# Attention rows stored whole and loaded in 512-byte pieces, w_ch1 in 128-column tiles, and new orders for the head and the middle

## Chip, core and metric

The kernel runs on one core of one Trainium2 chip. The metric is the device time of one execution in microseconds; the time given is the median of three runs. TensorE multiplies matrices, VectorE (DVE), ScalarE (ACT) and GpSimd (POOL) do the elementwise work, and SyncE (SP) issues most of the DMA transfers, ACT a few.

## The reference

Two parts follow each other, all in float32. The first is attention over a small memory, for 8 batches with 8 heads, 576 tokens, head size 64 and 32 memory slots:

```
a    = softmax over tokens of phi                  # 576 x 32 per head
k_m  = a^T k ;  v_m = a^T v                        # 32 x 64 per head
attn = softmax over slots of (q k_m^T / 8)         # 576 x 32 per head
x    = attn v_m, heads side by side                # 576 x 512 per batch
```

The second is a mixer on x:

```
u   = x + (relu(x^T w_tok1) w_tok2)^T              # over tokens, 576 -> 256 -> 576
out = u + relu(u w_ch1) w_ch2                      # over channels, 512 -> 1536 -> 512
```

## The kernel before

**Numbers.** Nearly all products run on operands split into a high and a low part (names with h and l), three products for one. The weights arrive as 64-bit words, from which ACT and DVE make the two parts in place (lines 825 to 859: raww for the token weights, rawc for the channel weights).

**Units of work.** A quad is half of a batch, four heads. Attention and the token mixer run by quad, 16 in all. The channel mixer runs by chunk of 512 tokens, 9 in all.

A quad's steps, in the order in which one waits for another:

- load phi, k and v, and q. For batches from 2 on the phi maxima are taken apart: load phi turned (l. 629), reduce it, store the maxima to DRAM (l. 638) and load them on all partitions as r (max_in, l. 644); GpSimd subtracts them (phi_sub, l. 647), and ACT takes the exponential (l. 446);
- k_m and v_m (kvp, l. 452), then the scores sp (l. 492). DVE turns them, so that a partition holds a token of a block of 32 for one head, and makes the softmax S with an exponential on ACT (l. 514) in between;
- two uses of S. Turned back it becomes aT, from which ACT and DVE make the operands a (l. 717, 722) for x. The token mixer instead needs tokens on partitions and heads side by side. S goes out to a DRAM tile, rows (rows_out, l. 545), and comes back in that layout (rows_in, l. 552 and 555, or 696 and 699 into the tile side). ACT copies it to the high part (nat_high, l. 703) and GpSimd makes the low part (nat_low, l. 711);
- Ap (attn^T w_tok1, l. 566), copied out as Ah by ACT (l. 737) and Al by DVE (l. 741); Rp (l. 749), then its relu parts Rh and Rl; at last the four tiles u (l. 768), each x and the token mixer summed in PSUM.

The channel mixer of chunk c makes cp (l. 146, with w_ch1), its relu parts hh and hl (l. 115, 118), and acc (l. 169, with w_ch2).

**Stages.** The head, to some 120 us, loads and converts all weights, runs the quads of batches 0 and 1 and the first chunk. The middle, to some 372 us, runs the 12 quads of batches 2 to 7 and chunks 1 and 2; u of later chunks is spilled to DRAM (l. 796). The middle also makes the sums of parts of w_ch1 and w_ch2 on which the last stage works, and stores them (class Sums: store_rest, l. 388, writes parts of w_ch1 as they are, store, l. 380, the sums; class Tops, l. 323). The last stage runs chunks 3 to 8 in three pairs with seven products of half size in place of eight (l. 292 and 2285), from u_p (l. 208), the spilled u.

**What sets the order.** All engines take their instructions in program order, and a planner at build time writes that order for head and middle. Each step has an engine, a duration, what it follows and the buffers (rooms) that it takes. The planner takes the engine that can start first, and on it, among the steps that can start within 0.1 us of that, the one with the highest rank; the program's order is that of the planned begins. In the head the ranks are the list RANKS; in the middle they come from a due time written beside each step (todo_at). Transfers are modelled by a line:

```
landed[eng] = max(landed.get(eng, 0.0), z.begin + 2.2) + 0.91 * z.move + 1.6 * (z is slow)
z.ready = max(landed[eng] + margin, z.end + z.tail)
```

so there is a line for each issuing engine, and a transfer counts as ready `margin` after its place in it, or `tail` after its issue. `slack` is added for steps on PE and SP, and `behind` limits how far SP's line may run ahead. In the middle margin is 4.0, slack 0.4 and behind 3.5; rows_in has a tail of 6.0, rows_out and the store of the maxima 2.4, the load of phi turned 4.0 or 8.0. The products of the channel mixer form one chain of steps of low rank.

Of the kernel before, what the change touches and what calls it, by code (L numbers as in the profile page):

```python
# [20 lines left out]
P = 128  # L21
# [7 lines left out]
def kernel(  # L29
# [97 lines left out]
    class Chunk:  # L127
# [6 lines left out]
        def mm_1(s, ps, f, only=None):  # L134
            w = slice(f % 2 * P, (f % 2 + 1) * P)
            c1h, c1l = c1[f // 2]
# [40 lines left out]
        def residual(s, a):  # L177
            if a == 0:
                s.o = wide(F32, "o" + s.n)
            nc.gpsimd.tensor_tensor(  # L180
# [161 lines left out]
    class Sums:  # L342
# [6 lines left out]
        def words(s):  # L349
            t = s.t = wide(F32R, f"sums{s.p}").rearrange("p a n -> p (a n)")  # L350
            s.v = t.rearrange("p (o x m) -> p o x m", o=4, x=2)
            for j in range(2):
                h, l = (f32(t[:, 2 * j : 2 * j + 2]).rearrange("p a (o n) -> p o a n", o=2) for t in c1[s.p])
# [73 lines left out]
    class Quad:  # L427
# [122 lines left out]
        def rows_in(s, tag, bufs):  # L550
            s.raw = sb.tile([P, NC, 4 * M], F32, tag=tag, name="raw" + s.n, bufs=bufs)
            nc.sync.dma_start(
                out=s.raw[:, :FULL], in_=s.rows[: FULL * P].rearrange("(c p) n -> p c n", p=P)
            )
            nc.sync.dma_start(out=s.raw[:TAIL, FULL], in_=s.rows[FULL * P :])
# [53 lines left out]
    class LateQuad(Quad):  # L609
# [84 lines left out]
        def rows_in(s):  # L694
            s.raw = side[0][:, :640].rearrange("p (c n) -> p c n", c=NC)
            nc.sync.dma_start(
                out=s.raw[:, :FULL], in_=s.rows[: FULL * P].rearrange("(c p) n -> p c n", p=P)
            )
            nc.sync.dma_start(out=s.raw[:TAIL, FULL], in_=s.rows[FULL * P :])

        def nat_high(s):
            s.nat_room()
            nc.scalar.copy(out=s.nh[:, :FULL], in_=s.raw[:, :FULL])  # L703
            nc.scalar.copy(out=s.nh[:TAIL, FULL], in_=s.raw[:TAIL, FULL])

        def nat_low(s, eng):
            for o, a, h in (
                (s.nl[:, :FULL], s.raw[:, :FULL], s.nh[:, :FULL]),
                (s.nh[TAIL:, FULL], s.raw[:TAIL, FULL], s.nh[:TAIL, FULL]),
# [194 lines left out]
    class PartC1:  # L904
# [10 lines left out]
        def load(s, raw):  # L915
            nc.sync.dma_start(out=raw.rearrange("p (a n) t -> p a (n t)", a=NKK), in_=w_ch1[s.f // 2])

        def dst(s):
            c1[s.f // 2] = tuple(
                sb.tile([P, NKK, 256], F32R, tag="c1", name=f"c1{x}{s.f}", bufs=NF) for x in "hl"  # L920
# [3 lines left out]
        def pick(s, x):  # L924
            return x.rearrange("p (a n) -> p a n", a=NKK)
# [37 lines left out]
    class Step:  # L963


        def __init__(s, eng, us, fn, after, take, use, move, port, other):
# [4 lines left out]
            s.fill, s.lands, s.not_before, s.tail = 0, False, 0.0, 1.0  # L971
# [13 lines left out]
    def plan(rank, ways, slow=None, slack=0.0, margin=0.85, behind=1e9):  # L985
# [10 lines left out]
        free, taken, landed, port = {}, {}, {}, 0.0  # L996
        left, done = [z for z in steps if not z.after], []

        def when(z):
            t = max(free.get(z.eng, 0.0), port if z.port else 0.0, z.not_before)  # L1000
            if z.eng == "SP":
                t = max(t, landed.get("SP", 0.0) - behind)
            for y in z.after:
                t = max(t, y.end if y.eng == z.eng and not (y.lands or y.move and y.eng == "ACT") else y.ready + slack * (z.eng in ("PE", "SP")))
# [20 lines left out]
        while left:  # L1025
# [1475 lines left out]
```

## Time and profile before

| | |
|---|---|
| median of three runs | 721.59 us (720.98 to 722.43) |
| the profiled execution | 722.78 us, of which span 721.0 us |
| TensorE busy | 708.4 us (98%) |
| DVE, ACT, GpSimd busy | 517.6, 371.4, 88.8 us |
| mean granted TensorE clock | 0.997 |
| DMA packets | 99200, of them 38985 under 512 bytes, 155.26 MB |

The span runs from the first instruction to the last of the profiled execution. A row of the table by stretches gives the stretch and its length in us, the busy time of PE (TensorE's products, with the number of them), PEld (its weight loads, beside the products), DVE, ACT and POOL, then the granted clock of TensorE as a share of 2.4 GHz, the mean busy share of the 16 DMA engines, and GB/s. A busy TensorE may still run at a low clock, so that column is read with it. In a timeline, the bracket at the end is the idle time of the engine before the instruction, and what ended it. The chain of waits is followed back from the last instruction, at each step to what released it; a DMA there runs from its issue to its landing. SPq is SP's queue, in which transfers are issued.

### The profile page before, as it was taken

How to read it: one execution, taken by the hardware profiler on the slowest of the kernel's cores; microseconds unless marked ns; L12 is line 12 of the kernel's file. 1: busy time of each engine (PE TensorE's matmuls, PEld its weight loads, DVE VectorE, ACT ScalarE, POOL GpSimd, SP SyncE). 2: the span in 40 equal slices, each digit the busy share in tenths (PEclk: the TensorE clock that was granted, in tenths of full speed). 3: DMA queues.
4: the chain of work that ended last, by engine and by line, in shares of the span. 5: the costliest groups of instructions: out<-in, count | busy, mean ns of one | idle time of the engine just before them, and what ended most of it. 6: DMA issues, size and time to landing. Idle time of an engine off the chain costs nothing.

```text
span 721.0 us, 11450 instructions
## 1 busy us (share of the span) xinstructions
PE 708.4 (98%) x4317; PEld 591.9 (82%) x4317; DVE 517.6 (72%) x854; ACT 371.4 (52%) x688; POOL 88.8 (12%) x80
## 2 busy tenths in 40 slices
PE   8999999999999998999999999999999999999998
PEld 7778888778888887888888888888888888888887
DVE  4999864877788676687965758966247977426983
ACT  6899765326564555445533465434345443436450
POOL 2143123021212402101400000000000000000000
PEclk9999999999999999999999999999999999999999
DMA  9967342789899999846437876184659065658202
GB/s 356 415 213 290 117 118 79 272 208 303 256 285 287 311 307 329 273 120 205 186 122 224 303 279 244 35 305 155 204 164 332 31 210 175 204 201 289 91 30 87
DMA packets 99200, 155.26 MB, mean 215 GB/s; under 512 B 38985, under 2 KB 65609, under 8 KB 94793
## 3 DMA queue, kind: packets, MB, share of 16 engines
q1 hardware_dynamic: 88632, 121.37, 50.0%
q10 hardware_dynamic: 10512, 33.17, 14.3%
q8 instruction: 34, 0.56, 0.3%
q14 instruction: 22, 0.17, 0.1%
HBM read 117.34 MB, written 37.16 MB: 214 GB/s over the span
## 4 chain that ended last, share of the span: by engine, by line
PE 82%; DMA 8%; DVE 5%; SPq 2%; ACT 1%; issue 1%; POOL 0%; ACTq 0%; POOLq 0%; DVEq 0%
PE ma L292 14%; PE acc L169 12%; PE cp L146 11%; PE mU L2285 10%; PE mB L2285 7%; PE mc L292 7%; PE u L768 5%; PE mD L2285 3%; PE mA L2285 3%; PE mb L292 3%; DMA side<-rows 2%; PE Ap L566 2%; DMA raww<-in_w_tok_dram 2%; PE kvp L452 1%; PE u L582 1%; DMA u_p<-spilled 1%
## 5 line engine op out<-in xcount | busy, mean ns | idle before, releaser
L169 PE MATMUL acc<-hh,c 128*128 128x512 f32 x288 | 100.6, 398 | 0.0
L169 PEld LDWEIGHTS acc<-hh,c 128*128 128x128 f32 x288 | 54.5, 189 | 13.1 <-issue 1.9
L169 PE MATMUL acc<-hl,c 128*128 128x512 f32 x144 | 56.7, 393 | 0.1
L146 PE MATMUL cp<-uh,c1h 128*128 128x512 f32 x144 | 52.4, 404 | 0.0
L146 PE MATMUL cp<-ul,c1h 128*128 128x512 f32 x144 | 50.5, 391 | 0.0
L146 PE MATMUL cp<-uh,c1l 128*128 128x512 f32 x144 | 50.4, 390 | 0.0
L2271 ACT CAST rT<-hid 128x512 fp32r<-128x512 f32 x54 | 32.0, 621 | 27.1 <-PE mB L2285 14.9
L2272 DVE TENSOR_TENSOR rT<-hid,rT 128x512 fp32r<-128x512 f32 x54 | 35.7, 684 | 7.0 <-ACT rT L2271 7.0
L2139 DVE TENSOR_TENSOR hid<-mb,hid 128x512 f32<-128x512 f32 x12 | 8.3, 692 | 41.8 <-ACT hid L2219 41.8
L115 ACT ACTIVATE hh<-cp 128x512 fp32r<-128x512 f32 x36 | 21.5, 598 | 29.9 <-PE cp L146 29.6
L711 POOL TENSOR_TENSOR nat<-side,nat 128x512 fp32r<-128x512 f32 (+1 forms) x24 | 23.5, 981 | 104.2 <-ACT nat L703 80.4
L2142 ACT ACTIVATE hid<-hid 128x512 f32<-128x512 f32 x24 | 15.2, 632 | 35.3 <-DVE hid L2139 35.3
L146 PEld LDWEIGHTS cp<-uh,c1h 128*128 128x128 f32 x144 | 26.6, 188 | 7.7 <-issue 3.6
L146 PEld LDWEIGHTS cp<-uh,c1l 128*128 128x128 f32 x144 | 27.0, 188 | 6.0
L169 PEld LDWEIGHTS acc<-hl,c 128*128 128x128 f32 x144 | 27.4, 190 | 4.9 <-DVE hl L118 0.6
L146 PEld LDWEIGHTS cp<-ul,c1h 128*128 128x128 f32 x144 | 27.1, 188 | 4.6
L118 DVE SCALAR_TENSOR_TENSOR hl<-cp,hh 128x512 fp32r<-128x512 f32 x36 | 24.7, 685 | 7.6 <-ACT hh L115 7.3
L778 ACT COPY side<-u 128x288 f32<-128x288 f32 (+1 forms) x44 | 17.0, 391 | 25.1 <-PE u L768 21.7
L2271 ACT CAST r<-hid 128x512 fp32r<-128x512 f32 x36 | 22.4, 623 | 14.3 <-PE mU L2285 5.4
L768 PE MATMUL u<-w2h,Rh 128*128 128x288 f32 x96 | 27.4, 301 | 0.6 <-ACT side L778 0.6
L2272 DVE TENSOR_TENSOR r<-hid,r 128x512 fp32r<-128x512 f32 x36 | 24.7, 685 | 4.6 <-ACT r L2271 4.3
L292 PE MATMUL ma<-xrest_p,unit 128*128 128x512 f32 x108 | 27.4, 389 | 0.0
(381 smaller groups left out, 1926.4 us busy)
## 6 DMA issues: line engine op xcount, KB each, us to landing
unit<-sums ACTq DMA_DIRECT2D x54, 512.0 KB, 4.7
kv<-in_kv_dram SPq DMA_DIRECT2D x12, 1300.0 KB, 7.8
rawc<-in_w_ch_dram SPq DMA_DIRECT2D x12, 1024.0 KB, 4.9
q<-in_q_dram SPq DMA_DIRECT2D x16, 576.0 KB, 5.1
sums<-sums SPq DMA_DIRECT2D x12, 512.0 KB, 6.1
u_p<-spilled SPq DMA_DIRECT2D x6, 1024.0 KB, 6.5
phi<-in_phi_dram SPq DMA_DIRECT2D x16, 320.0 KB, 7.7
unit<-sums ACTq DMA_DIRECT2D x18, 256.0 KB, 3.0
```

Of the source, the lines that this page charges most:

```text
L115: nc.scalar.activation(out=h, in_=ps, func=AF.Relu)
L118: nc.vector.scalar_tensor_tensor(out=l, in0=ps, scalar=0.0, in1=f32(h), op0=ALU.max, op1=ALU.subtract)
L146: nc.tensor.matmul(ps, l[:, a, w], r[:, a], start=n == 0, stop=n == len(mm) - 1)
L169: nc.tensor.matmul(ps, l_[f // 2][:, f % 2, a * P : (a + 1) * P], r[:, w], start=f == start and x == 0, stop=f == end - 1 and x == 2,)
L292: nc.tensor.matmul(ps, l, r, start=first and n == 0, stop=n == len(mm) - 1, skip_group_check=not first,)
L711: eng.tensor_tensor(out=o, in0=a, in1=f32(h), op=ALU.subtract)
L768: nc.tensor.matmul(s.up[db, hf][:, :HALF], a, r, start=x == 0, stop=x == len(mm) - 1)
L778: nc.scalar.copy(out=side[0][:, o + n : o + HALF], in_=ps[:, n:HALF])
L2142: nc.scalar.activation(out=to, in_=x, func=AF.Relu)
L2271: nc.scalar.copy(out=t[:, 0], in_=x)
L2272: nc.vector.tensor_tensor(out=t[:, 1], in0=x, in1=f32(t[:, 0]), op=ALU.subtract)
L2285: nc.tensor.matmul(s.banks[room][a][:, w], l_[:, a * P : a * P + P], r_, start=not (p or x) and name in ("11", "T1", "21", "T4"), stop=p = ...
```

## The change

- rows_out stores S as it lies, 128 rows of 2304 bytes, in one transfer. rows_in becomes take_rows: four transfers, each of 32 partitions, in pieces of 512 bytes, and two for the last 64 tokens, in pieces of 128 bytes. The partitions then hold the tokens in another order, so w_tok1 and the first batch's q are laid out by it on the host, and the first batch's a_get puts its columns back. nat_high and nat_low read with the heads outside and write as before.
- w_ch1's tiles become two blocks of 128 columns, each with the four channel groups behind each other; the host lays it out so. A product reads its 128 columns from one block. store_rest writes runs of 2048 and 1024 bytes in place of 512.
- In the planner one line holds the transfers of all engines, the extra for a slow step is gone, and a step can have a cushion, time that is kept between it and what it follows. Costs and sizes of transfers are set anew (rows_out 0.45 in place of 2.2 us of SP, rows_in 2.8 in place of 1.0), the tails above are gone, and the sums and the first loads of the last stage may start at other times.
- The head's first loads come in another order, and RANKS is a new list. The middle's ranks are a list of 972 numbers, PLACES, in place of the due times, with slack 0.3976, margin 1.0393 and behind 5.1679.

Parameters that would move GpSimd's work to DVE (PHI_ON, LOW_ON, O_ON) or delay a residual (O_AT) are added, and set so that nothing moves.

```diff
-                    nc.tensor.matmul(ps, l[:, a, w], r[:, a], start=n == 0, stop=n == len(mm) - 1)
+                    nc.tensor.matmul(ps, l[:, a], r[:, a], start=n == 0, stop=n == len(mm) - 1)
...
-                for j, src in ((0, h[:, :, :P]), (3, h[:, 2:, P:])):
+                for j, src in ((0, h[:, 0]), (3, h[:, 1, 2:])):
                     n = src.shape[1] * P
-                    to = s.to[:, j, x * n : x * n + n].rearrange("p (a n) -> p a n", n=P)
-                    nc.sync.dma_start(out=to, in_=src)
+                    nc.sync.dma_start(out=s.to[:, j, x * n : x * n + n], in_=src.rearrange("p a n -> p (a n)"))
...
         def rows_out(s):
-            s.rows = dram.tile([S, 4 * M], F32, name="rows" + s.n, tag="rows", bufs=2)
-            for i in range(4):
+            s.rows = dram.tile([P, S], F32, name="rows" + s.n, tag="rows", bufs=2)
+            nc.sync.dma_start(out=s.rows, in_=s.S.rearrange("p a m -> p (a m)"))
...
+        def take_rows(s, t):
+            n, by_token = FULL * P, s.rows.rearrange("(i t) n -> t i n", t=32)
+            main = t[:, :n].rearrange("p (i n) -> p i n", i=4)
+            last = t[:TAIL, n:].rearrange("p (i m) -> p i m", i=4)
+            for g in range(4):
+                nc.sync.dma_start(out=main[32 * g : 32 * g + 32], in_=by_token[:, :, P * g : P * g + P])
+            for g in range(2):
                 nc.sync.dma_start(
-                    out=s.rows[:, i * M : (i + 1) * M].rearrange("(a t) m -> t a m", t=32),
-                    in_=s.S[32 * i : 32 * i + 32],
+                    out=last[32 * g : 32 * g + 32], in_=by_token[:, :, n + M * g : n + M * g + M]
                 )
...
+            s.raw = main.rearrange("p i (c m) -> p c i m", c=FULL), last
...
-            nc.scalar.copy(out=s.nh[:, :FULL], in_=s.raw[:, :FULL])
+            nh, _ = s.nats()
+            nc.scalar.copy(out=nh[:, :FULL], in_=s.raw[0])
...
-                landed[eng] = max(landed.get(eng, 0.0), z.begin + 2.2) + 0.91 * z.move + 1.6 * (z is slow)
-                z.ready = max(landed[eng] + margin, z.end + z.tail)
+                line = max(line, z.begin + 2.2) + 0.91 * z.move
+                z.ready = max(line + margin, z.end + z.tail)
...
-        a.l_phi, loads[0], c.l_phi, loads[1], a.l_k, a.l_q, c.l_k, c.l_q, a.l_v, c.l_v, loads[3], loads[2], loads[4],
+        a.l_phi, loads[0], c.l_phi, a.l_k, loads[1], a.l_q, c.l_k, a.l_v, c.l_q, loads[3], loads[2], c.l_v, loads[4],
...
-    SUMS_AT = [30, 60, 90, 120, 150, 180]
+    SUMS_AT = [10, 35, 60, 85, 110, 135]
...
-        z = do(6.5, "SP", 2.2, qd.rows_out, w, use=[S_], move=0.7)
-        z.lands, z.tail = True, 2.4
-        z = do(9, "SP", 1.0, qd.rows_in, z, sided, take=[raw], use=[side_room], move=0.8)
-        z.tail = 6.0
+        z = do(6.5, "SP", 0.45, qd.rows_out, w, use=[S_], move=0.81)
+        z.lands = True
+        z = do(9, "SP", 2.8, qd.rows_in, z, sided, take=[raw], use=[side_room], move=1.18)
         h = z = do(12, "ACT", 0.95, qd.nat_high, z, take=[nat], use=[raw])
+        z.cushion = 1.5 * CUSHION
...
-    order = plan(key, dict.fromkeys(steps, 0), None, SLACK, 4.0, BEHIND)
+    order = plan(dict(zip(steps, PLACES, strict=True)), dict.fromkeys(steps, 0), 0.3976, 1.0393, 5.1679)
...
-    c1 = moe_w_ch1[ch].reshape(4, P, ff // 256, 256).transpose(2, 1, 0, 3)
+    c1 = moe_w_ch1[ch].reshape(4, P, ff // 256, 2, P).transpose(2, 1, 3, 0, 4).reshape(ff // 256, P, -1)
```

CUSHION is 0.9; the exponential of phi has twice that, and the sums' high part once. In `first_loads`, a and c are the quads of the first batch, and loads[0] to loads[4] are w_tok1, its last rows, the two halves of w_tok2 and the first part of w_ch1.

## Rows read from the trace of the kernel before

**Rows 1.** The page, busy us with share of span and instructions
```profile
PE 708.4 (98%) x4317; PEld 591.9 (82%) x4317; DVE 517.6 (72%) x854; ACT 371.4 (52%) x688; POOL 88.8 (12%) x80
```

**Rows 2.** Busy time by stretches, columns as told above
```profile
0.00:50.00 50.00, 46.31 (x456) 39.44 (x457) 39.62 (x67) 39.29 (x68) 12.26 (x24) 1.00 0.89 352
20.00:40.00 20.00, 19.54 (x155) 15.84 (x155) 19.66 (x28) 18.46 (x33) 4.59 (x2) 1.00 1.02 408
118.00:372.00 254.00, 248.46 (x1924) 209.25 (x1923) 192.95 (x351) 124.41 (x279) 58.78 (x47) 0.99 0.79 247
260.00:284.00 24.00, 21.07 (x168) 17.99 (x167) 14.78 (x27) 11.62 (x29) 3.97 (x4) 0.93 1.01 357
320.00:372.00 52.00, 50.28 (x289) 44.54 (x288) 42.79 (x65) 29.01 (x58) 11.71 (x8) 1.00 0.51 172
372.00:721.00 349.00, 345.63 (x1542) 286.83 (x1540) 230.95 (x360) 153.18 (x256) 0.00 (x0) 1.00 0.54 185
280.00:283.00 3.00, 2.95 (x10) 2.67 (x11) 2.97 (x6) 0.66 (x2) 0.00 (x0) 0.50 1.02 363
```

**Rows 3.** Waits of TensorE over the span: us in total, times, longest
```profile
PE Rp L749 <- ACT Ah L737: 2.6, 1, 2.6
PE Rp L749 <- DVE Al L741: 1.7, 1, 1.7
```

**Rows 4.** Chain of waits ahead of 280 us: start, us, what
```profile
268.97 6.58 DMA r<-top
...
275.71 1.58 POOL phi L647
...
279.62 0.38 ACT Ah L737
```

**Rows 5.** Timeline of TensorE, 281 to 285 us: start, us, instruction
```profile
281.07 0.63 PE L169 MATMUL acc<-hh,c 128*128 128x512 f32 x1
281.50 0.63 PE L169 MATMUL acc<-hl,c 128*128 128x512 f32 x1
...
284.12 0.39 PE L169 MATMUL acc<-hh,c 128*128 128x512 f32 x1
284.35 0.40 PE L146 MATMUL cp<-uh,c1h 128*128 128x512 f32 x1
```

**Rows 6.** Timelines of ACT and DVE, 350 to 354 us
```profile
350.46 1.05 ACT L275 CAST xqT_p<-u_p 128x1024 fp32r<-128x1024 f32 x1
...
353.75 0.42 DVE L741 TENSOR_TENSOR Al<-Ap,Ah 128x256 fp32r<-128x256 f32 x1
```

**Rows 7.** Lines 545 and 696: issue min/median/max ns; line 545 to landing
```profile
L545 SPq DMA_DIRECT2D rows<-S x56: 302/546/3404, 66.7 to 325.9; - x56
...
DMA to landing us min/median/max: 2.0/4.7/9.4
...
L696 SPq DMA_DIRECT2D side<-rows x12: 360/490/846, 147.2 to 336.7; - x12
```

**Rows 8.** DMA queues from 324.3 to 328.5 us: packets, MB, share of engines
```profile
q1 hardware_dynamic: 2368, 0.30, 47.5%
```

**Rows 9.** DMA queues from 317.2 to 320.5 us, rows_in among larger pieces
```profile
q1 hardware_dynamic: 902, 0.76, 75.4%
```

**Rows 10.** ACT's waits for the rows (118 to 372), its cast, a strided one
```profile
ACT nat L703 <- DMA side<-rows: 5.5, 5, 2.2
...
L703 ACT CAST nat<-side 128x512 fp32r<-128x512 f32 x11 | 6.8, 619 | 5.6 <-DMA side<-rows 5.5
...
45.59 0.68 ACT L855 CAST c<-rawc 128x512 fp32r<-128x512 f32 x1
```

**Rows 11.** The head: DVE's and ACT's timelines, and SP's waits to 22 us
```profile
18.05 0.48 DVE L1148 SCALAR_TENSOR_TENSOR vb<-vp,col,mask 128x256 f32<-128x256 f32 x1 [1.77 <-PE vp L1251]
...
20.20 0.85 ACT L825 ACTIVATE raww<-raww,mask 128x576 f32<-128x576 uint32 x1 [3.28 <-DMA raww<-in_w_tok_dram]
...
SPq L1269 <- DMA raww<-in_w_tok_dram: 1.3, 1, 1.3
```

More of the change, by code (lines that the diff above doesn't have):

```diff
@@ L915, in load @@
         def load(s, raw):
[L916 removed]
+            nc.sync.dma_start(out=raw.rearrange("p n t -> p (n t)"), in_=w_ch1[s.f // 2])
         def dst(s):
             c1[s.f // 2] = tuple(
[L920 removed]
+                sb.tile([P, 2, NKK, P], F32R, tag="c1", name=f"c1{x}{s.f}", bufs=NF) for x in "hl"
             )
@@ L970, in __init__ @@
             s.begin = s.end = s.ready = None
-            s.fill, s.lands, s.not_before, s.tail = 0, False, 0.0, 1.0
+            s.fill, s.lands, s.not_before, s.tail, s.cushion = 0, False, 0.0, 1.0, 0.0
             s.held = [room for room in (*take, *use) if room.tags[0][0] in ("at", "ch")]
@@ L983, with plan @@
     OVERLAP = {"ACT": 0.09, "DVE": 0.07}
-    def plan(rank, ways, slow=None, slack=0.0, margin=0.85, behind=1e9):
+    def plan(rank, ways, slack=0.0, margin=0.85, behind=1e9):
         then = {z: [] for z in steps}
@@ L995, in plan @@
         needs = {z: len(z.after) for z in steps}
-        free, taken, landed, port = {}, {}, {}, 0.0
+        free, taken, line, port = {}, {}, 0.0, 0.0
         left, done = [z for z in steps if not z.after], []
@@ L1001, in when @@
             if z.eng == "SP":
-                t = max(t, landed.get("SP", 0.0) - behind)
+                t = max(t, line - behind)
             for y in z.after:
-                t = max(t, y.end if y.eng == z.eng and not (y.lands or y.move and y.eng == "ACT") else y.ready + slack * (z.eng in ("PE", "SP")))
+                t = max(t, y.end if y.eng == z.eng and not (y.lands or y.move and y.eng == "ACT") else y.ready + z.cushion + slack * (z.eng in ("PE", "SP")))
             more = {}
@@ L1371, in a_get @@
             s.aT = sb.tile([P, S], F32, tag="ah", name="aT" + s.n, bufs=2)
-            for x in range(2):
-                w, t = s.turned(x)
-                nc.scalar.copy(out=s.aT[:, w], in_=t)
+            n = FULL * P
+            nc.scalar.copy(
+                out=s.aT[:, :n].rearrange("p (g c t) -> p c g t", g=4, c=FULL),
+                in_=s.tp[0].rearrange("p c (g t) -> p c g t", g=4),
+            )
+            nc.scalar.copy(out=s.aT[:, n:], in_=s.tp[1][:, :TAIL])
         def mm_A(s, ps):
@@ L1829 @@
     )
-    LATER, SOON = -1e4, 1e4
+    engines = {"POOL": nc.gpsimd, "DVE": nc.vector}
     key = {}
@@ L2023, in first_layer @@
         hidden[c, f], parts[c, f] = (hh, hl), [h, l]
+        late_o = c == 2 and O_AT
         if f == NF - 1:
@@ L2026, in first_layer @@
                 z = todo_at(
-                    -50, "POOL", 1.45, lambda a=a: mixer(c).residual(a), z, take=[] if a else [o_rooms[c]],
+                    O_AT if late_o else -50, O_ON, 1.45 if O_ON == "POOL" else 0.87,
+                    lambda a=a: mixer(c).residual(a, engines[O_ON]),
+                    *([z] if a or not late_o else [t_low, *second_u]), take=[] if a else [o_rooms[c]],
                     use=u_rooms[c] + ([o_rooms[c]] if a else []), port=True,
@@ L2042, in second_layer @@
         if f == NF - 1:
-            z = todo_at(-50, "SP", 0.45, lambda: chunks[c].store(), *(added[c, a] for a in range(NKK)), use=[o_rooms[c]], move=2.9)
+            z = todo_at(-50, "SP", 0.45, lambda: chunks[c].store(), *(added[c, a] for a in range(NKK)), use=[o_rooms[c]], move=2.71)
             z.lands = True
@@ L2060 @@
         z = todo_at(t0 + 3, "ACT", 1.15, x.high, z, use=[w])
+        z.cushion = 1.0 * CUSHION
         z = todo_at(t0 + 5, "DVE", 1.25, x.low, z, use=[w], port=True)
-        z = todo_at(t0 + 6, "SP", 0.9, x.store, z, use=[w], move=2.9)
+        z = todo_at(t0 + 6, "SP", 0.9, x.store, z, use=[w], move=2.8)
         z.lands = True
@@ L2118 @@
             z = todo_at(
-                180 + x + 20 * p, "ACT" if x == 8 else "DVE", (1.1, 1.25)[x - 8] if x > 7 else 0.6 if x < 4 else 0.43,
+                190 + x + 20 * p, "ACT" if x == 8 else "DVE", (1.1, 1.25)[x - 8] if x > 7 else 0.6 if x < 4 else 0.43,
                 lambda p=p: tops_go(p), z, take=[] if x else ct, use=ct if x else [], port=x != 8,
             )
-            z.not_before = 180
+            z.not_before = 190
+        todo_at(201 + 20 * p, "SP", 0.9, None, z, use=ct, move=2.8).lands = True
     held = [room("c1", NF) for n in range(AHEAD)]
     for n in range(AHEAD):
-        todo_at(195 + n, "ACT", 0.1, load_unit, *summed, take=[held[n]])
-    todo_at(1e5, "END", 0, None, *steps, use=[*held, *uv, *t_rooms, *sum(xr.values(), [])])
-    order = plan(key, dict.fromkeys(steps, 0), None, SLACK, 4.0, BEHIND)
+        z = todo_at(218 + 5 * n, "ACT", 0.4, load_unit, *summed, take=[held[n]], move=1.4)
+        z.not_before = 212 + 5 * n
+    todo_at(1e5, "END", 0, None, *steps, use=[o_rooms[2], *held, *uv, *t_rooms, *sum(xr.values(), [])])
+    PLACES = (
[48 rows of a table added]
+    )
+    order = plan(dict(zip(steps, PLACES, strict=True)), dict.fromkeys(steps, 0), 0.3976, 1.0393, 5.1679)
     for z in order:
```

99 lines of the change are left out of this document (48 added, 51 removed), and 91 rows, old and new, of tables (PLACES, RANKS).

## The prediction

> **What bounds the kernel now.** First the busy line of the page: TensorE is busy 708.4 us of a span of 721.0 [rows 1]. Then the table by stretches [rows 2], which shows where it is not: 3.69 us of the first 50, 5.54 us between 118 and 372 (2.93 of them from 260 to 284, 1.72 from 320 on), and 3.37 after 372, which is the last store behind the last product. From 372 on the products otherwise follow each other without a gap, and nothing of that code changes. So the change can act on the head and on the middle (118 to 372) alone.
>
> Next the waits of TensorE [rows 3]: two long ones, both of the attention product Rp, 2.6 us for Ah and 1.7 us for Al. The chain of waits tells where the first comes from [rows 4]: the load of the maxima, r, was 6.58 us under way; GpSimd's subtraction on phi waited for it, then ACT's exp of phi, in whose queue stood the copies up to Ah. In that stretch the DMA engines are busy 1.01 of the time [rows 2]. The stall costs more than its length: from 280 to 283 the granted clock is 0.50, that is 1.2 GHz in place of 2.4, and products of 512 columns start 0.43 us apart where they start 0.23 apart a little later [rows 2, 5]. From 280.05 to the first start at the quick pace some 3.15 us pass, and half of that is lost: 1.57 us. The second wait has nothing to do with a transfer: ACT made an operand of the next phase (xqT_p), and Al came late on DVE [rows 6].
>
> So the middle loses 5.5 us idle and 1.6 us to the slow clock, 7.1 us. That is all it can give back.
>
> **The change part by part.**
>
> *Rows out, 12 quads in the middle and 2 in the head.* Before, four transfers of 128-byte pieces. Issuing them took SP 56 x a median of 0.546 us, up to 3.4 us for one [rows 7]; where the queue carried nothing else, the four held all 16 engines for 0.475 x 4.2 = 2.0 us, for 0.30 MB [rows 8]. After, one transfer of 128 pieces of 2304 bytes. At the head's rate (352 GB/s at a share of 0.89, so 395 GB/s while busy [rows 2]) it takes 0.75 us: 1.25 us of DMA time and three SP issues less per quad. The bounds are 0 (pieces cost nothing) and 1.25; I take 1.25, as the head's loads are in pieces of that size.
>
> *Rows in.* Before two transfers, after six: four of 64 KB in 512-byte pieces as before, two of 16 KB in 128-byte pieces (256 in all, where there were 64 of 512). DMA time: 256/2304 of those 2.0 us is 0.2 us, for what took at most that, so 0 to +0.2. SP issues: two at about half a microsecond become six [rows 7], so the last piece is issued about 2.0 us later. With three issues saved ahead (1.6 us) and a shorter transfer, the way from the end of the softmax to the rows in SBUF is about level: -1 us where the queue is full, +0.8 where it is empty. I count it at 0; what covers it is the product chain that TensorE runs between attention steps, and where that is gone a microsecond late is a microsecond stalled.
>
> *Sums.* The pieces in which w_ch1's parts are written grow from 512 to 1024 and 2048 bytes. Six times 768 KB take 2.0 us each at 395 GB/s; at the rate of rows 8 (150 GB/s) they would take 5.2, at that of the nearest mixture (0.76 MB at 75.4% of 3.3 us, 902 pieces, so 305 GB/s [rows 9]) 2.6. The gain is 0 to 3.2 us of DMA time each; I take 0.5, by the nearest. With rows out (12 x 1.25) the middle's queue is relieved by some 17 us of the 201 it is busy (0.79 of 254 [rows 2]). The sums may also start 10 us after the middle's begin in place of 30, so part of their transfers leaves the full stretch.
>
> *Copies that read in another order* (nat_high, nat_low, the first batch's a_get): as many, with as many elements. The plain cast of 512 columns takes 0.619 us, the nearest one with a stride 0.68 [rows 10]: +0.06 x 12 on ACT, which works 124 of the middle's 254 us [rows 2]. 0 on the path, +0.7 if that cover is gone. The products and weight loads on w_ch1 read 128 columns as before: 0.
>
> *Head.* The new order of the first loads puts both halves of w_tok2 ahead of the second quad's values (650 KB, 1.7 us at 395 GB/s), and the first quad's values ahead of the second's q (576 KB, 1.5 us). Now ACT idles 3.28 us before w_tok2, and DVE 1.77 us before the product of the first quad's values [rows 11]; from 20 to 40 DVE is busy 19.66 of 20 [rows 2]. A head that is as long as its DVE work gets shorter by what DVE starts earlier: at most 1.7. I take 1.3, as the second quad's values come 1152 KB or 3.0 us later; their product ran early, and if that cover fails it costs up to 1.5. Bounds -1.7 and +0.5, the ranks of the head being new as well.
>
> *Order of the middle.* All 972 steps take a new rank; due times no longer decide. The plan reckons a landing 1.04 us behind the line in place of 4.0, drops the paddings of 2.4 to 8 us on single loads, and puts 0.9 to 1.8 us ahead of what follows three loads on ACT. With one line for all transfers it can see the crowding behind rows 4. Of the 4.5 us lost there (2.93 + 1.57) I take 3.5 back; of the other 2.6 us 0.6, since the wait for Al is a matter of ACT's order; and +0.5 for waits that the thinner padding lets in. Lateness doesn't add up: once TensorE has stalled, all that follows has that much more slack. Middle: -3.6, bounds -7.1 and +6.7 (rival C).
>
> Sum: -1.3 - 3.6 = -4.9 us. The profiled execution took 722.78 us (its span and 1.78 around it), so 717.9 in its place; it lies 1.19 over the median of 721.59, which gives 716.7.
>
> **Rivals.** A is the forecast. B: the loss moves. Transfers land earlier, but the thinner padding puts their users earlier too, and as much stalls elsewhere. For it: ACT already waits 5.5 us in five waits for the rows [rows 10], and 2.6 us of the loss is no transfer's. Against it: the queue is freed by 8%. Head -1.3, middle 0: 720.3, with 719.5 to 722.
>
> C: slower, by the six pieces on SP. SP keeps eight transfers open: in the head the tenth issue waits 1.3 us, until the second has landed [rows 11]. Six small ones fill that window, and each quad's last rows are issued 2.0 us later; nat_high on ACT waits for them with all ACT's copies out of PSUM behind it, then GpSimd, Ap, Rp. It decides where the plan's cushion of 1.35 us is used up, in the full stretch first. Three stalls like the one of 2.57 in place of one, and one more stretch at half clock: +5.1 + 1.6 = +6.7, with the head's -1.3 +5.4: 727.0. Against it: four transfers issued together were through in 2.0 us of engine time [rows 8], so pieces do overlap.
> The Trainium skill's page "DMA: Bandwidth & Descriptors" speaks for C: its section "Rules for kernel authors" says that transfers to disjoint partition halves serialize and that one over 128 partitions should be used, and its section "Anatomy of one DMA" gives about 2 us fixed for each. Were these paid one behind the other, six pieces would be an estimated 12 us for 4 now, and C would come true or worse. The trace agrees with 2 us as the time to land (minimum 2.0 in rows 7), not as time in a line, so the rule adds little to C's chance.
>
> D: all is given back: -7.1 - 1.7 = -8.8, 712.8. For it: a middle with products enough to fill every gap needs no stall.
>
> **How the numbers follow.** A 0.55 (own range 714 to 719.8), B 0.17, C 0.15, D 0.13. A measurement of this kernel can tell 0.2%, 1.4 us, from no change. Faster by more: A and D, a fifth of B, less A's upper tail: 0.68. Within: 0.13, mostly B. Slower: C and the upper ends of B and A, 0.19. The range reaches from D's 712.5 to 723.5, above B; below it some 0.06 is left out, above it most of C.
>
> **What would show it.** Right: SP's rows out are one issue of about 0.5 us; DMA packets fall from 99200 to some 65000 (14 x 2176 and 6 x 1024 fewer, 14 x 192 more); no stretch at clock 0.50 between 118 and 372; TensorE idle there under 3 us; ACT's wait for w_tok2 ends 1.7 us sooner and the mixer's first product starts 1 us or more earlier. Wrong: new waits of Ap or Rp behind nat_high that end with the rows' landing (C), as much idle in other places (B), or a first mixer product no earlier than now.

## The result, and the profile after

The changed kernel took 730.77 us (median of 6 runs, 728.75 to 734.87) beside 721.38 us for the kernel before: a ratio of 1.0132, 95% interval 1.0104 to 1.0161. It is slower by some 9.4 us where 4.9 fewer were forecast, and 7.3 us above the range. The profiled execution took 730.58 us, of which span 728.6.

Two marks in the trace cut the span into head, middle and last stage: the second chunk's first cp product, and the first product of the mixer's pairs. The first came at 126.45 us before and at 124.84 after, the second at 371.80 and 379.52. So the head is 1.6 us shorter, the middle 9.3 us longer (245.35 and 254.68), and the last stage 0.1 us shorter. Marks, waits and stretches, here and below, are those of one profiled execution of each kernel.

Lines of the page after, answering to [rows 1] and to the packets in the table of before:

```profile
PE 707.4 (97%) x4305; PEld 590.4 (81%) x4305; DVE 519.5 (71%) x857; ACT 369.7 (51%) x686; POOL 84.4 (12%) x79
...
DMA packets 65503, 155.26 MB, mean 213 GB/s; under 512 B 10536, under 2 KB 28584, under 8 KB 61096
...
q1 hardware_dynamic: 54936, 121.37, 47.0%
```

TensorE works as much as before; the span is longer. A third of the packets is gone, as forecast.

Busy time by stretches after (columns as in [rows 2]; the first rows answer to it), and under it the two stretches of before that [rows 2] lacks:

```profile
0.00:50.00 50.00, 45.15 (x463) 37.34 (x464) 39.75 (x69) 40.53 (x72) 12.97 (x24) 1.00 0.89 353
118.00:372.00 254.00, 240.86 (x1869) 202.06 (x1868) 185.60 (x342) 118.68 (x268) 54.77 (x44) 0.99 0.72 244
118.00:260.00 142.00, 133.79 (x1067) 111.03 (x1066) 102.86 (x197) 62.62 (x145) 31.67 (x26) 0.98 0.76 256
260.00:284.00 24.00, 23.85 (x181) 20.22 (x181) 17.95 (x34) 12.18 (x26) 2.14 (x2) 1.00 0.88 310
284.00:320.00 36.00, 32.38 (x282) 26.72 (x288) 23.21 (x41) 16.24 (x39) 7.91 (x6) 1.00 0.76 251
320.00:372.00 52.00, 50.84 (x350) 44.09 (x347) 41.58 (x71) 27.64 (x60) 13.04 (x10) 1.00 0.52 176
232.90:239.70 6.80, 5.43 (x23) 5.43 (x24) 3.42 (x8) 3.17 (x9) 3.12 (x3) 0.50 0.86 331
```

```profile
118.00:260.00 142.00, 141.11 (x1171) 117.05 (x1170) 108.99 (x213) 67.14 (x157) 37.78 (x31) 1.00 0.86 263
284.00:320.00 36.00, 36.00 (x303) 29.67 (x302) 26.39 (x48) 16.64 (x39) 5.30 (x5) 1.00 0.78 222
```

The middle read as stretch less busy time. From 260 to 284, TensorE is idle 0.15 us where it was 2.93, and from 320 to 372 1.16 where it was 1.72: both places that I meant to mend are mended, by 2.8 and 0.6 us. But from 118 to 260 it is idle 8.21 us where it was 0.89, and from 284 to 320 3.62 where it was 0. In all 13.14 us for 5.54: +7.6. The rest is clock: 6.8 us at 0.50 with 5.43 busy, where before there were 3.4 with 3.05; half of the difference is 1.2 us. That is 8.8 of the 9.3. Over the 254 us the DMA engines are busy 0.72 in place of 0.79, 183 us for 201: the relief of 17 us that I reckoned is there.

TensorE's waits in the middle after (us in total, times, longest), answering to [rows 3]:

```profile
PE u L772 <- ACT side L782: 4.2, 1, 4.2
PE kvp L682 <- ACT T L679: 4.1, 2, 2.9
PE kvp L450 <- DMA kv<-in_kv_dram: 2.8, 2, 2.1
```

The longest, and the chain of waits that led to it (start, us, what), answering to [rows 4]:

```profile
225.37 6.24 DMA side<-rows
...
232.07 0.04 ACT nat L706
...
232.59 0.29 ACT nat L707
232.88 0.31 ACT vh L475
233.19 0.58 ACT S L512
233.78 0.15 ACT kb L686
233.92 0.30 ACT side L782
...
234.27 1.81 PE u L772 x6
```

The last pieces of the attention rows were issued at 224.9 and landed at 231.6. ACT waited for them with nat_high (L706), and behind it in ACT's queue stood vh, an exponential (S), kb and the copy of u out of PSUM (L782), for which TensorE's next product u waited. TensorE stood from 230.07 to 234.27. This is the chain that I gave to rival C, once; the other long waits are of other kinds: kv landing 8.5 us after its issue, and u_p, which was 6.35 us under way and held up DVE, then T.

The six pieces don't make this chain. order_only, a kernel of the next section with the same order and the rows back in two pieces, has it at the same place: the rows were issued at 225.31, also landed 6.24 us later, and TensorE waited 2.1 us for the same copy of u (after 1.7 us for Rh just before).

```profile
225.31 6.24 DMA side<-rows
...
233.49 0.30 ACT side L778
...
233.84 2.28 PE u L768 x11
```

### The profile page after: what moved, and what is told of

Same layout as the page of the kernel before. It is cut to its first block, busy times and chain, and to the rows that moved or that the text cites. A ratio compares the mean times of both kernels' runs of the same rounds, so it can differ in the third digit from the quotient of the medians.

```text
span 728.6 us, 11479 instructions
## 1 busy us (share of the span) xinstructions
PE 707.4 (97%) x4305; PEld 590.4 (81%) x4305; DVE 519.5 (71%) x857; ACT 369.7 (51%) x686; POOL 84.4 (12%) x79
## 2 busy tenths in 40 slices
DMA packets 65503, 155.26 MB, mean 213 GB/s; under 512 B 10536, under 2 KB 28584, under 8 KB 61096
## 4 chain that ended last, share of the span: by engine, by line
PE 77%; DMA 13%; DVE 5%; SPq 2%; ACT 1%; issue 1%; POOL 0%; ACTq 0%; POOLq 0%
PE ma L291 13%; PE mU L2347 10%; PE cp L145 9%; PE acc L168 9%; PE mB L2347 7%; PE mc L291 7%; PE u L772 4%; PE mD L2347 3%; PE mA L2347 3%; PE mb L291 3%; DMA sums<-sums 3%; PE Ap L572 2%; DMA raww<-in_w_tok_dram 2%; DMA r<-top 1%; DMA kv<-in_kv_dram 1%; PE u L588 1%
## 5 line engine op out<-in xcount | busy, mean ns | idle before, releaser
L118 DVE SCALAR_TENSOR_TENSOR hl<-cp,hh 128x512 fp32r<-128x512 f32 x36 | 24.6, 683 | 13.7 <-ACT hh L115 13.4
L653 POOL TENSOR_TENSOR phi<-phi,r 128x640 f32<-128x640 f32 x11 | 17.4, 1579 | 99.3 <-DMA r<-top 91.5
L772 PE MATMUL u<-w2l,Rh 128*128 128x288 f32 x96 | 27.5, 301 | 0.0
```

Of the source, the lines that this page charges most:

```text
L118: nc.vector.scalar_tensor_tensor(out=l, in0=ps, scalar=0.0, in1=f32(h), op0=ALU.max, op1=ALU.subtract)
L653: eng.tensor_tensor(out=s.pt, in0=s.pt, in1=s.r.rearrange("p (i m) -> p i m", i=4) .unsqueeze(2) .to_broadcast([P, 4, NC, M]), op=ALU.subt ...
L772: nc.tensor.matmul(s.up[db, hf][:, :HALF], a, r, start=x == 0, stop=x == len(mm) - 1)
```

## The experiments

The middle's length below is the time between the two marks above. "Wide" is the reckoning of the plan before (margin 4.0 behind the line, tails of 2.4 to 8 us), "thin" that of the new plan (1.04, no tails). What a plan expects of a transfer can be read off its steps: the time from a step's planned begin to the time at which the plan counts it as landed.

**Halves of the change.** Four kernels of one set, two more later. The new transfers and layouts with the old orders (take_rows, nats, store_rest and the host's part as after; ranks, due times and the plan as before):

```diff
-            for i in range(4):
...
-                    in_=s.S[32 * i : 32 * i + 32],
+            nc.sync.dma_start(out=s.rows, in_=s.S.rearrange("p a m -> p (a m)"))
...
-                    nc.tensor.matmul(ps, l[:, a, w], r[:, a], start=n == 0, stop=n == len(mm) - 1)
+                    nc.tensor.matmul(ps, l[:, a], r[:, a], start=n == 0, stop=n == len(mm) - 1)
```

> The kernel before with the new transfers and layouts alone (rows out in one transfer, rows in in six, w_ch1 in 128-column tiles, the host's layouts), planned as before, so the order of all steps is the old one. Theory O (the new order of the middle with its thin padding loses the 9.3 us): 718 to 721.5, the middle no longer than before (245.3 us from the second chunk's first product to the first pair's). Theory T (the six returning pieces lose them): 726 to 731, with new waits of ACT's nat_high for the rows and TensorE idle behind them.

Measured: 726.85 us, ratio 1.0066 (1.004 to 1.0092). Part of that is the head, made for other transfers: the clock was 0.51 from 18.8 to 25.8 us, the first cp came 2.1 us later, and the second chunk began 1.5 us later. The middle took 248.1 us, 2.7 more than before, and the stall of [rows 3] was still there (1.8 us for Ah), with r 7.15 us under way where it took 6.58 [rows 4]. A queue with 15 us less work (a share of 0.73 for 0.79 over 118 to 372) did not bring this load sooner. The time lies in theory T's range, but its sign is missing: ACT waited 3.5 us for the rows, where it had waited 5.5 [rows 10].

The reverse, old transfers with both new orders:

```diff
-    order = plan(key, dict.fromkeys(steps, 0), None, SLACK, 4.0, BEHIND)
+    order = plan(dict(zip(steps, PLACES, strict=True)), dict.fromkeys(steps, 0), 0.3976, 1.0393, 5.1679)
```

> The changed kernel with the transfers and layouts of before, planned as the changed one. Theory O: as slow as the changed kernel or slower, 730 to 736, since rows in 128-byte pieces land later than the plan reckons. Theory T: 719 to 722, as before or better by the head's 1.6 us.

Measured: 728.49 us, 1.0102 (1.0073 to 1.0131), the middle 251.1 us: 1.5 us under theory O's range and far above T's. The new order loses without any of the new transfers.

New transfers and the new head, the middle planned as before:

```diff
-    order = plan(dict(zip(steps, PLACES, strict=True)), dict.fromkeys(steps, 0), 0.3976, 1.0393, 5.1679)
+    order = plan(key, dict.fromkeys(steps, 0), None, SLACK, 4.0, BEHIND)
```

> The new transfers and layouts with the head's new loads, costs and ranks; the middle planned as before. Theory O: the head's 1.6 us less than layout_only, so 716.5 to 720, the fastest of the four. Theory T: 1.6 less than layout_only there too, so 724 to 729. If the head's gain doesn't carry through a middle that is planned apart from it, both give layout_only's time.

Measured: 724.26 us, 1.0027 (1.0006 to 1.0048), the middle 246.5 us. From here to the changed kernel only the middle's plan differs: 1.05% or 7.6 us. But 724.26 is again in T's range, not in O's: the transfers lose something too (see head_only below).

The changed kernel with the margin put back, ranks as they are:

```diff
-    order = plan(dict(zip(steps, PLACES, strict=True)), dict.fromkeys(steps, 0), 0.3976, 1.0393, 5.1679)
+    order = plan(dict(zip(steps, PLACES, strict=True)), dict.fromkeys(steps, 0), 0.3976, 4.0, 5.1679)
```

> The changed kernel with one number of the middle's plan back: a landing is reckoned 4.0 us behind the line in place of 1.04; ranks, costs and cushions stay. Theory O in the form 'thin padding': most of the 9.3 us come back, 721 to 725. Theory O in the form 'the ranks themselves': 728 to 735, as the ranks were made for 1.04. Theory T: 728 to 731, nothing of the transfers being changed.

Measured: 737.29 us, 1.0215 (1.0195 to 1.0235), above all three ranges. It decides nothing between them: ranks found for 1.04 leave gaps in a plan for 4.0, whose own end lies 24.6 us later. Between the two marks it took 261.7 us, 6.0 less than planned, where the thin plan took 11.6 more.

Then the new head alone, and with it earlier due times, to mend the stall of [rows 4] by the old plan's own means (max_out, load_phi, max_in, phi_sub and the exponential 4 us earlier too, load_turned 6):

```diff
-            y = do(-34, "DVE", 0.85, qd.phi_max, y, use=[turned])
+            y = do(-38, "DVE", 0.85, qd.phi_max, y, use=[turned])
```

> The kernel before with the head alone changed: its first loads, its ranks, its costs of rows out and rows in. Transfers, layouts and the middle's plan are those of before. The second chunk's first product started 1.6 us earlier in the changed kernel (124.84 against 126.45). If the head's gain carries through a middle whose order is the same, 719.5 to 721; if the transfers of the middle, met at another moment by TensorE's clock and the queue, swallow it, 721.5 to 724.

> head_only, and in the middle the due times of the phi maxima, phi and its exponential 4 us earlier (6 for the turned phi), as the change writes them down where they no longer decide. Paddings and transfers as before. If the stall at 277 us of the kernel before was a matter of when r is asked for, and not of how much the queue carries, it goes or shrinks: 716 to 719. If the queue decides, r is as late as before: 719.5 to 722.

Measured: 722.04 us (0.9989, 0.997 to 1.0007) and 721.57 (0.9985, 0.997 to 1.0). The head's 0.8 us can't be told from nothing, and the due times add nothing that can. They did move the loss: TensorE's wait for Ah is 2.8 us in head_only's trace and 0.8 in head_due's, and its waits for the copies of u are 1.7 and 3.0 us, with rows 11.08 us under way ahead of one of them. So the stall went with the moment at which r is asked for, as the expectation had it, but the time of the whole did not.

So the 1.32%, by these ratios, divide into -0.11% for the head, +0.38% or 2.7 us for the new transfers (layout_head over head_only), and +1.05% or 7.6 us for the middle's plan; with the old transfers that plan costs 1.13% or 8.2 us (order_only over head_only).

**Wide or thin, by one search.** The changed plan differs from the old in more than its padding: it has searched ranks. So I searched ranks for four plans in one way (random changes of the list, kept where the planned end of TensorE's last step fell), until each had no gap. All have the new head and SP's 3.5 us ahead; two have the old transfers, two the new, with their new costs on SP. The thin ones have 1.0393 in place of 4.0 and no tails.

```diff
-    order = plan(key, dict.fromkeys(steps, 0), None, SLACK, 4.0, BEHIND)
+    order = plan(dict(zip(steps, PLACES, strict=True)), dict.fromkeys(steps, 0), None, SLACK, 4.0, BEHIND)
```

> The kernel before with the new head; the order of the middle is not by due times but by one place per step, found by the same kind of search as the other three kernels of this set, against the old plan's paddings (4.0 us behind the line, 2.4 to 8 us on single loads). Planned without a gap: 244.1 us of middle. Theory T (thin padding is what loses): as the head alone, 719 to 723. Rival P (a searched order as such loses, whatever it was searched against, because due times spread the loads better): 726 to 729.

> As the one before, old transfers, but searched against thin paddings: 1.04 us behind the line, none on single loads, no cushions. Planned without a gap as well: 244.3 us. Theory T: 5 us or more above its twin with wide paddings, 726 to 730. Rival P: as its twin. Rival L (only the new transfers lose): as the head alone, 719 to 723.

> The new transfers and head, SP's issues and the transfers' lengths reckoned as the new plan has them, searched against wide paddings. Planned without a gap: 244.1 us. Theory T with a small loss of the new transfers: 722 to 725. Rival L: 725 to 728, and the same with thin paddings. If the new transfers are a gain that the old due times only could not use: 719 to 721.

> As the one before, searched against thin paddings (1.04 us, none on single loads, no cushions). Planned without a gap: 244.1 us. Theory T: 5 us or more above its twin, 727 to 732, like the changed kernel. Rivals P and L: as its twin.

Measured, in that order: 719.71, 731.63, 723.11, 722.99 us. With the old transfers wide wins (0.9957) and thin loses (1.0121), as theory T (here: thin paddings lose) has it; with the new ones there was no difference, which T had excluded. Either the new transfers make a thin plan safe, or a thin plan is a matter of luck. Four more lists, from other starts, told these apart; two of them with the changed kernel's own reckoning, so that they differ from it by ranks alone, or (after_b35, the diff) by those and 3.5 us of SP's issuing ahead in place of 5.17.

```diff
-    order = plan(dict(zip(steps, PLACES, strict=True)), dict.fromkeys(steps, 0), 0.3976, 1.0393, 5.1679)
+    order = plan(dict(zip(steps, PLACES, strict=True)), dict.fromkeys(steps, 0), 0.3976, 1.0393, 3.5)
```

> The changed kernel with nothing but the middle's ranks searched once more, from another start, against the same reckoning (1.04 us behind the line, the cushions, 5.17 us of issuing ahead). Planned without a gap: 243.9 us. Theory T (the reckoning is too thin, any order found against it loses): 726 to 733. Rival X (this one list of ranks was unlucky): 719 to 724.

> As the one before, searched with 3.5 us of issuing ahead of the line in place of 5.17, as the old plan has it; planned without a gap: 243.9 us. Theory T: as its twin, 726 to 733. Rival Q (issuing further ahead puts urgent transfers behind others in SP's queue): 3 us or more below its twin, 720 to 724.

> New transfers, thin paddings, no cushions, 3.5 us ahead: a second list of ranks from another start for the kernel that took 723.0 us. Planned without a gap: 244.0 us. If thin paddings lose by chance, now here and now there: anywhere from 721 to 733, and not the same as its twin. If the new transfers make thin paddings safe: 721 to 724 again.

> Old transfers, thin paddings: a second list of ranks for the kernel that took 731.6 us. Planned without a gap: 244.1 us. Theory T: 724 to 734. Rival X: as the head alone, 719 to 723.

Measured: 728.54, 728.99, 734.65 and 742.80 us; the first two are in theory T's range, the others above every range given. So it is luck, and mostly bad. How far SP issues ahead (rival Q) made no difference between the first two; as their lists differ as well, one such pair says little. A second list of the wide kind, run with the last set:

> Old transfers, new head, a second list of ranks searched against the wide paddings from another start; planned without a gap: 244.1 us. Theory T: 718 to 722, like its twin at 719.7, while second lists against thin paddings lay 11 us apart. If wide paddings only had luck: 724 to 735.

Measured: 721.23 us, 0.998 (0.9966 to 0.9993). All plans side by side. Both lengths of the middle are counted between the two marks; the expectations above count a plan from its own zero, 1.72 us ahead of the second chunk's first product. "Under way" is the mean time from issue to landing of the 116 steps of the middle that SP issues, as planned and as the trace of that kernel has it; "longer" counts those of the 116 that were longer under way than their plan had it. The ratio is to the kernel before. Times are medians; the profiled execution behind a measured middle lay up to 2.3 us from them.

| plan | transfers | middle planned | measured | under way planned | measured | longer | time | ratio |
|---|---|---|---|---|---|---|---|---|
| wide: before | old | 243.0 | 245.3 | 7.9 | 6.2 | 23 | 721.4 | 1 |
| wide: head_only | old | 243.0 | 245.4 | 7.9 | 6.3 | 20 | 722.0 | 0.9989 |
| wide: layout_head | new | 243.0 | 246.5 | 7.9 | 6.1 | 19 | 724.3 | 1.0027 |
| wide: s_old_wide | old | 242.4 | 242.7 | 7.9 | 6.5 | 24 | 719.7 | 0.9957 |
| wide: s_old_wide2 | old | 242.4 | 246.0 | 7.9 | 6.4 | 25 | 721.2 | 0.9980 |
| wide: s_new_wide | new | 242.3 | 245.9 | 8.1 | 6.2 | 19 | 723.1 | 0.9998 |
| thin: after | new | 243.1 | 254.7 | 5.6 | 6.2 | 68 | 730.8 | 1.0132 |
| thin: order_only | old | 243.1 | 251.1 | 5.6 | 6.1 | 66 | 728.5 | 1.0102 |
| thin: after_again | new | 242.2 | 252.1 | 5.7 | 6.2 | 65 | 728.5 | 1.0077 |
| thin: after_b35 | new | 242.2 | 253.7 | 5.2 | 6.3 | 76 | 729.0 | 1.0077 |
| thin: s_new_thin | new | 242.4 | 244.9 | 5.0 | 6.0 | 74 | 723.0 | 0.9994 |
| thin: s_new_thin2 | new | 242.3 | 257.8 | 5.0 | 6.2 | 78 | 734.7 | 1.0161 |
| thin: s_old_thin | old | 242.5 | 254.4 | 5.0 | 6.1 | 78 | 731.6 | 1.0121 |
| thin: s_old_thin2 | old | 242.4 | 269.2 | 4.9 | 6.0 | 65 | 742.8 | 1.0259 |

Every plan ends within a microsecond of the others by its own account. On the chip a transfer was about 6 us under way whatever the plan said. Plans that had reckoned 8, which 19 to 25 of the 116 steps overran, came out 0.4 to 3.6 us above their account; plans that had reckoned 5 to 6, which 65 to 78 overran, 2.6 to 27 above. Counted by lists, six of the seven that were found against thin paddings lost 0.77% or more, and none of the three found against wide ones lost. That s_new_thin lost nothing, with 74 overrun, shows that many late transfers needn't cost time; what decides which order pays for them stays open. The slowest list, s_old_thin2: its longest waits of TensorE in the middle and the chain to the first (columns as above):

```profile
PE u L768 <- ACT side L778: 4.2, 1, 4.2
PE kvp L676 <- ACT T L673: 3.9, 1, 3.9
PE u L768 <- DVE ul L195: 3.6, 1, 3.6
PE kvp L676 <- DVE side L1147: 3.3, 1, 3.3
```

```profile
360.69 5.76 DMA rows<-S
...
366.59 2.83 DMA side<-rows
...
369.50 0.46 ACT nat L703
...
370.04 0.28 ACT nat L704
370.32 0.30 ACT side L778
...
370.67 0.76 PE u L768 x2
```

It is again the way of the rows, here by the old transfers: out 5.76 us, back 2.83, nat_high, and the copy of u behind it on ACT. The first wide plan with the same transfers (s_old_wide) has no wait of this kind longer than 0.6 us; its longest is that for Al, which [rows 3] has too. The second (s_old_wide2) has three waits for copies of u, 3.1 us in all, the longest 2.3. Those of s_old_wide:

```profile
PE Rp L749 <- DVE Al L741: 1.8, 1, 1.8
PE u L768 <- ACT side L778: 0.6, 1, 0.6
```

**Where the relief of the queue went.** The list of s_old_wide once more, the same order to the step and the same planned costs, with the parts of the new transfers: sw_c1 has w_ch1's tiles, sums and store_rest as after, sw_rows has rows_out, take_rows, nats, a_get and the host's order of tokens, sw_both has all of it. The core of the first:

```diff
-                sb.tile([P, NKK, 256], F32R, tag="c1", name=f"c1{x}{s.f}", bufs=NF) for x in "hl"
+                sb.tile([P, 2, NKK, P], F32R, tag="c1", name=f"c1{x}{s.f}", bufs=NF) for x in "hl"
```

> The kernel that took 719.7 us (new head, middle searched against wide paddings), with the same order to the step, and of the new transfers the layout of w_ch1 alone, so that its parts are written out in pieces of 1024 and 2048 bytes. If the relief that I predicted is real (0.5 us of the queue for each of six writings) and nothing else changes: 717 to 720. If the wide plan had no use for it: 719 to 721. If this layout is what costs the new transfers their 3 us: 721.5 to 724.

> The same order again, and of the new transfers the attention rows alone: out in one transfer, back in six. By my prediction (1.25 us of the queue less per quad, the way there and back about level): 716 to 720. If the six pieces on SP are what costs (the last one issued some 2 us later, and what stands behind them in SP's queue with it): 721.5 to 724.

> The same order with both parts. From the two pairs so far (new transfers against old at wide paddings: +2.7 and +3.4 us): 721.5 to 724. If those differences came from where each plan happened to be tight, not from the transfers: 718 to 721.

Measured: 718.63 us (0.9941, 0.9925 to 0.9956), 723.10 (0.9996, 0.9982 to 1.001) and 721.02 (0.9985, 0.9971 to 0.9998), where none of it gave 0.9957 (0.9934 to 0.9981). The tiles of w_ch1 gain 0.16%, which can't be told from nothing; the rows lose 0.39%, 2.8 us, more than the two half-intervals together by root of squares (0.27%), and with the tiles in both (sw_both over sw_c1) 0.44%; sw_both's time lies at the upper end of the lower of its two ranges. The share of the DMA engines over 118 to 372 fell from 0.794 to 0.783 by the tiles and to 0.746 by the rows, 2.8 and 12 us of relief for the 3 and 15 that I had put in, and the mean time under way fell from 6.5 to 5.9 us by the rows. The rows themselves came sooner: their way out took 3.9 us (median of the middle's twelve, from the first issue to the last landing) in place of 6.8, the way out and back 12.1 in place of 14.5. But TensorE's waits in s_old_wide name no transfer, so there was nothing to gain from it.

In SP's queue, six issues in hold it 3.5 us a quad (median) where two held it 1.3, and one issue out 0.4 where four held it 3.6; its waits for the rows to land before they are loaded grow from 3.0 to 10.0 us over the middle. What this can cost is seen in the same stretch of the same order; with the rows:

```profile
285.89 3.03 SPq L554 DMA_DIRECT2D side<-rows  x4
289.02 0.85 SPq L556 DMA_DIRECT2D side<-rows  x2
289.97 0.38 SPq L633 DMA_DIRECT2D q<-in_q_dram  x1
290.46 0.84 SPq L380 DMA_DIRECT2D sums<-sums  x2
291.39 1.33 SPq L629 DMA_DIRECT2D kv<-in_kv_dram  x1
```

and without (s_old_wide):

```profile
285.83 0.36 SPq L696 DMA_DIRECT2D side<-rows  x1
286.28 1.11 SPq L699 DMA_DIRECT2D side<-rows  x1
287.45 0.57 SPq L625 DMA_DIRECT2D q<-in_q_dram  x1
288.11 0.86 SPq L380 DMA_DIRECT2D sums<-sums  x2
289.02 1.25 SPq L621 DMA_DIRECT2D kv<-in_kv_dram  x1
```

The quad's rows begin to be issued at the same time, 285.89 and 285.83. Two issues hold SP until 287.39, six until 289.87, and the load of kv behind them goes out at 291.39 in place of 289.02: 2.4 us later. In sw_rows it was waited for:

```profile
PE kvp L452 <- DMA kv<-in_kv_dram: 2.1, 1, 2.1
```

The trace of s_old_wide has no such wait. So here the six pieces cost by the time that SP takes to issue them, and what pays is the next load in its queue, not the rows. That this one stall is the whole of the 2.8 us was not shown. One profile has it, where it is 2.1 of the 2.2 us between the two profiled executions; in sw_both the six pieces begin at 284.60, the load of kv goes out at 289.69, and TensorE waits for it 0.3 us. The Trainium skill's page "DMA: Bandwidth & Descriptors" says in its section "Rules for kernel authors" that issuing from several engines brings no bandwidth but saves issue time on the sequencer; issuing the rows from another engine wasn't tried here.

**The best version.** sw_c1 beats both kernels: 4.1 us less than the 722.76 us of the kernel before in its set. It has the new head and the new tiles of w_ch1, the old rows, and a middle searched against the old, wide reckoning, by the better of the two lists of that kind.

## Why the prediction was wrong, step by step

**What bounds the kernel: right.** The two losses of the middle were where I read them, and both were mended in place. That the rest of the middle ran without a loss before (0.89 us idle) came of its order: with another the same transfers lost 8 us (order_only).

**Head: the size right, the way there not shown.** Forecast -1.3 us; the second chunk begins 1.6 us sooner, though the first cp only 0.8, and TensorE is idle 4.85 us of the first 50 where it was 3.69 [rows 2]. ACT's wait for w_tok2, which ended at 20.20 [rows 11], ends 1.9 us sooner (forecast 1.7). The line of ACT's timeline after:

```profile
18.29 0.83 ACT L829 ACTIVATE raww<-raww,mask 128x576 f32<-128x576 uint32 x1 [2.30 <-DMA raww<-in_w_tok_dram]
```

In the times of whole runs (head_only) it is 0.1%, which can't be told from nothing, and loads and ranks were changed together.

**Rows out and sums: the terms right, their worth wrong.** Line 542 is one issue of 0.3 us where four took 2.2 [rows 7] (the answer for the line, duration min/median/max):

```profile
L542 SPq DMA_DIRECT2D rows<-S x14: 319/335/1158, 66.5 to 347.5; - x14
...
DMA to landing us min/median/max: 2.1/7.1/8.6
```

65503 packets for the forecast 65000, and 18 us less of the queue for 17. The way of a quad's rows out was 6.8 us (median) and is 6.9, but that compares two orders; in one order it fell to 3.9 (sw_rows). Relief of a queue is time only where something on the path waits for it.

**Rows in: "the way about level" was wrong for the rows and left out the queue.** In one order the rows came 2.4 us sooner (14.5 and 12.1), where I had counted 0. But I looked at when the last piece lands and not at what stands behind six issues on SP; by sw_rows the new rows cost about 2.8 us. In the changed kernel SP, done with one issue out, waits for it to land, with all later loads behind the wait. SP's wait after:

```profile
SPq L552 <- DMA rows<-S: 31.2, 9, 6.7
```

Before, the same wait (line 696) came to 1.5 us. Part of the growth is the new transfers (10.7 in layout_only), part the order (11.0 in order_only), and it isn't a loss by itself: s_new_thin has 23.6 us of it and took no longer than the kernel before. Rival C had the issues on SP right. Its chain is in the changed kernel, but in order_only too, with the rows in two pieces, so the pieces don't make it. That its price (727.0) came near the result was luck: order_only lost 1.13%, 8.2 us, over head_only with the old pieces.

The 2 us fixed for each transfer, which the prediction takes from the Trainium skill's page, stand in a section there on transfers that GpSimd issues; here SP issues them. The runs show no such 12 us: in one order the six pieces took 5.6 us from the first issue to the last landing, as the two did (medians of sw_rows and s_old_wide).

**"Order of the middle": the step that failed.** I took 3.5 of 4.5 us back and 0.6 of 2.6; measured were 2.8 of idle time and 0.6, and the half-clock stretch there is gone: right. To that I put "+0.5 for waits that the thinner padding lets in". This term measured +10.9 us of idle time in stretches that had 0.9, and one longer stretch at half clock; the plan's part of that, with transfers and head as they are, is 7.6 us (layout_head). The error was to take the planner's reckoning for a description of the chip. Padding looked like waste; but a searched plan with 4.0 us of it ends as early as one with 1.04 (242.3 and 242.2 us), at TensorE's floor, so thinning it could win nothing, and it took away what covers a transfer that takes longer than reckoned: 68 of 116 did so in the changed kernel, 23 before. I could have seen this from [rows 4] and [rows 7]: ways of 2.0 to 9.4 us for one and the same line.

**"Lateness doesn't add up": wrong as a bound.** With s_old_thin2 at +27 us it adds up over a dozen quads. Counted from the first mark, its transfers are issued 8.1 us behind the plan by the median and land 9.5 behind it; in the changed kernel these are 6.4 and 6.0, and in the kernel before -0.4 and -1.8, ahead of the plan.

What of the reckoning matters most, the margin or the tails, stays open: they were only changed together. The cushions didn't save the changed kernel's reckoning, nor does leaving them out explain the loss: lists with them (after, after_again, after_b35) and without (s_old_thin, s_new_thin2) both lost. What one line for all engines' transfers is worth by itself stays open as well.

## What to carry to other kernels

A plan that is at the floor by its own account can't be improved by thinner paddings, only made fragile: compare planned and measured times under way, transfer by transfer, before touching them, and judge an order by how late a transfer may be, not by its end. Test a searched order with a second list from the same search; one list says little (723 and 735 us from the same reckoning). Count a split transfer by its issues, and charge them to whatever stands next in that queue.

## What the runs showed of the hardware

The granted clock showed only its two levels, the lower one (1.2 GHz) for example from 279.8 to 283.2 us before and from 232.9 to 239.7 in the changed kernel. It came with stalls, but not by their length: with the one of 2.57 us before [rows 3] and the one of 4.20 after, not with the one of 2.90 after, up to 295.98, behind which the clock stayed at 1.00. In layout_only it fell in the head without a long stall: 1.59 of 2.8 us busy from 16.0 to 18.8, then 0.51 from 18.8 to 25.8, with TensorE busy for all of it. The mean time under way stayed at 5.9 to 6.6 us over all kernels of the table and the last set, at shares of the DMA engines from 0.71 to 0.80; single steps took 1.5 to 13 us.
